# Storing two of 64 chunks in parts that run on different numbers of DMA engines

## The chip, the cores and the metric

The kernel runs on one core of one Trainium2 chip. The core has TensorE (PE, matmuls; its weight loads are listed as PEld), VectorE (DVE), ScalarE (ACT), GpSimd (POOL) and SyncE (SP), and 16 DMA engines that carry every transfer between HBM and the core's SBUF, whichever engine issued it. The metric is device time in microseconds (us), the median of three runs. One further execution was recorded by the hardware profiler; the durations in this document come from it.

## The reference

The input `x` is one image of 512 x 512 pixels with 192 channels in bf16, and the output has the same shape. The convolution has a 1 x 1 kernel, so each pixel is treated by itself: its 192 channels are four groups of 48, and each group is multiplied by its own 48 x 48 matrix.

```python
# k = 1, G = 4, Cg = 48, pad = 0
xg = x.reshape(B, H, W, G, Cg)
out = einsum('bhwgc,gcd->bhwgd', xg, w[0, 0])   # then back to (B, H, W, 192)
```

100.66 MB are read and as many written; the arithmetic beside them is small.

## The kernel before

**Chunks.** The 262,144 pixels are cut into 64 chunks of 4096 pixels. In a chunk each of the 128 SBUF partitions holds 32 neighbouring pixels, so one partition's row is 32 x 192 bf16 values, 12,288 bytes, contiguous in HBM. A chunk is 128 rows, 1.5 MB. Chunk n uses buffer n mod 5 of the five input buffers `x_sb` and of the five output buffers `o_sb`.

**Loads.** SP issues one load per chunk (L160), in order. From the sixth on, the load of chunk n first waits until PE has transposed all of chunk n-5, which was in the same buffer.

**Compute.** A chunk is worked in eight groups of four pixels per partition. PE transposes a group (six transposes, L192), DVE copies them from PSUM to SBUF (L242), PE multiplies by a block-diagonal weight (six matmuls, L214), and ACT writes the result to `o_sb` as bf16 (L285); in three groups of ten DVE and ACT do one half each (L249, L282). PE runs up to two groups of transposes ahead. The weights are built at the start from `w`.

**Stores.** ACT issues one store per chunk (L269), in `store(n)`, after the chunk's last group. ACT's program is in order and has this shape: at the first group of chunk n it waits until the store of chunk n-5 has landed on all its DMA engines (`st_sem`), and the store of chunk n-1 comes after that, two groups into chunk n. So the store of chunk n-1 is not issued before that of chunk n-5 has landed. DVE waits on the same semaphore before it first writes `o_sb` for a chunk.

**Queues.** Loads are on the queue called q1, stores on q10. A chunk's 128 rows are dealt out evenly, eight to each of the 16 DMA engines, and each engine counts the semaphore up by one when its rows are done; a whole transfer counts 16. `store_parts(n)` already allows a store to be made in several transfers; before the change it returns one part of 128 rows for every chunk.

Of the kernel before, what the change touches and what calls it, by code (L numbers as in the profile page):

```python
# [24 lines left out]
PPC = 32  # L25
NB = 5
TAIL = (32, 32, 32, 32)
RELIEF = ()
RELIEF_ROWS = ((0, 128),)
NXP = 4  # L30
NOB = 4
NXS = 4
# [21 lines left out]
def bass_standalone__grouped__vision_kernel(nc, x, w, out):  # L54
# [49 lines left out]
        return ap[pix0[n]:pix0[n] + 128 * s, :].rearrange("(p i) c -> p (i c)", p=128)  # L104

    def store_parts(n):
        return RELIEF_ROWS if n in RELIEF else ((0, 128),)

    st_total, acc = [], [0] * NB
    for n in range(n_chunks):  # L110
        acc[n % NB] += 16 * len(store_parts(n))
        st_total.append(acc[n % NB])
# [4 lines left out]
    with ExitStack() as es:  # L117
# [136 lines left out]
        def _(act):  # L254
# [4 lines left out]
            def store(n):  # L259
                b = n % NB  # L260
                g = g1[n] - 1
                if g < GT:
                    wq.wait(mm_done, g + 3)
                else:
                    wq.wait(actT_sem, actT_cnt(g))
                    wq.wait(ev2T_sem, dveT_cnt(g))
                dst = rows_view(of, n)
                for (r0, r1) in store_parts(n):
                    act.dma_start(dst[r0:r1, :], o_sb[b][r0:r1, 0:sizes[n] * C]).then_inc(st_sem[b], 16)  # L269
# [51 lines left out]
```

## Time and profile before

| | us |
|---|---|
| median of three runs | 494.51 (491.5, 494.51, 494.85) |
| the profiled execution's own time | 494.62 |
| its span, first to last instruction | 492.9 |
| PE / ACT / DVE busy | 415.4 / 349.0 / 348.0 |
| packets of q1 and q10, share of 16 engines' span | 48.3% and 48.2% |
| mean rate over the span | 409 GB/s |

The span is 1.7 us shorter than the execution's own time. A "packet" is what one DMA engine moves at a time: here one row of 12,288 bytes, or the 4-byte count of the semaphore.

The trace also records when each of the 16 engines counted its part of a transfer as done. These are some transfers, in us from the start of the span, with the engines sorted by the time at which they were done (the trace does not give the engines' numbers):

| transfer | issued | first engine | 9th | 15th | last engine |
|---|---|---|---|---|---|
| store of chunk 20 | 155.56 | 177.45 | 178.49 | 179.91 | 184.93 |
| store of chunk 42 | 322.55 | 338.38 | 339.42 | 341.64 | 353.13 |
| store of chunk 45 | 345.52 | 360.30 | 361.32 | 363.57 | 376.09 |
| load of chunk 51 | 348.96 | 363.99 | 364.62 | 367.25 | 379.92 |
| store of chunk 57 | 437.27 | 448.09 | 449.10 | 451.99 | 467.76 |
| load of chunk 63 | 440.53 | 451.31 | 452.40 | 455.68 | 471.52 |
| store of chunk 58 | 444.94 | 453.61 | 454.25 | 457.51 | 473.56 |
| store of chunk 62 | 474.35 | 479.24 | 479.35 | 479.86 | 488.68 |
| store of chunk 63 | 480.45 | 485.34 | 485.45 | 485.53 | 492.31 |

A column is read downwards: how fast that engine advances. A row is read across: how far the engines are apart.

### The profile page before, as it was taken

To read this page: it belongs to the slowest core of one execution; us is meant where nothing else is said; L and a number is where in the kernel's file an instruction comes from. 1 tells how busy PE (TensorE), PEld (TensorE's weight loads), DVE (VectorE), ACT (ScalarE), POOL (GpSimd) and SP (SyncE) were. 2 spreads that over 40 slices of the span, in tenths; PEclk is the share of its full clock that TensorE was granted. 3 is DMA by queue.
4 is the path that set the end of the run, shared out by engine and by line. 5 is a ranking of instruction groups with operands and counts; after the bars stand their busy time and mean duration, and the time that the engine had idled before them with its cause. 6 is when DMAs were issued, how large, how long until landed. Compare 5 with 4: busy or idle time off the path is not lost.

```text
span 492.9 us, 15013 instructions
## 1 busy us (share of the span) xinstructions
PE 415.4 (84%) x6154; PEld 390.5 (79%) x6154; DVE 348.0 (71%) x666; ACT 349.0 (71%) x513; POOL 1.3 (0%) x8
## 2 busy tenths in 40 slices
PE   4888999999999888888888888888888888888880
PEld 4788999999989887787777877878778787787770
DVE  2767888888888776776776767677667767777760
ACT  1757888888888767677677776766767667676680
POOL 1000000000000000000000000000000000000000
PEclk9989999999999999999999999999999999999995
DMA  8999999999999999999999999999999999999563
GB/s 342 398 428 426 427 429 427 428 428 428 429 428 429 430 429 430 429 430 428 427 430 430 429 429 429 430 428 427 429 428 430 428 427 430 430 430 430 213 266 144
DMA packets 18658, 201.56 MB, mean 409 GB/s; under 512 B 2256, under 2 KB 2256, under 8 KB 2256
## 3 DMA queue, kind: packets, MB, share of 16 engines
q1 hardware_dynamic: 9424, 100.69, 48.3%
q10 hardware_dynamic: 9216, 100.67, 48.2%
q8 instruction: 7, 0.11, 0.1%
q14 instruction: 11, 0.09, 0.0%
HBM read 100.68 MB, written 100.66 MB: 409 GB/s over the span
## 4 chain that ended last, share of the span: by engine, by line
DMA 67%; PE 2%; ACT 1%; ACTq 0%; issue 0%
DMA out_dram<-o_sb 67%; PE o_ps L214 1%; ACT o_sb L285 1%; PE xT_ps L192 1%; ACTq L269 0%; ACT o_sb L282 0%; ACTq L47 0%
## 5 line engine op out<-in xcount | busy, mean ns | idle before, releaser
L285 ACT CAST o_sb<-o_ps 128x768 bf16<-128x768 f32 x359 | 280.1, 799 | 99.9 <-PE o_ps L214 65.4
L242 DVE COPY xT_sb<-xT_ps 128x768 bf16<-128x768 bf16 x512 | 282.3, 554 | 89.4 <-PE xT_ps L192 84.3
L214 PE MATMUL o_ps<-wt,xT_sb 128*128 128x144 bf16 (+1 forms) x3072 | 297.5, 233 | 46.9 <-PEq L169 40.5
L192 PE MATMUL xT_ps<-ident,x_sb 128*128 128x128 bf16 x3072 | 256.7, 220 | 10.0 <-PEq L169 4.9
L214 PEld LDWEIGHTS o_ps<-wt,xT_sb 128*128 128x128 bf16 x3072 | 210.9, 98 | 64.4 <-issue 51.5
L192 PEld LDWEIGHTS xT_ps<-ident,x_sb 128*128 128x128 bf16 x3072 | 196.8, 98 | 17.2 <-issue 17.1
L249 DVE CAST o_sb<-o_ps 128x384 bf16<-128x384 f32 x153 | 84.6, 553 | 32.9 <-DMA out_dram<-o_sb 20.0
L282 ACT CAST o_sb<-o_ps 128x384 bf16<-128x384 f32 x153 | 73.4, 480 | 30.7 <-DMA out_dram<-o_sb 19.6
L178 PE MATMUL o_ps<-w_sb,esel 48*128 48x48 bf16 x10 | 0.6, 209 | 7.3 <-DMA w_sb<-in_w_dram 7.3
L236 DVE CAST wt<-o_ps 128x480 bf16<-128x480 f32 x1 | 0.7, 658 | 7.9 <-PE o_ps L178 7.9
L178 PEld LDWEIGHTS o_ps<-w_sb,esel 48*128 48x128 bf16 x10 | 0.5, 110 | 7.3 <-issue 7.3
L285 ACT ACT_TABLE_LOAD x1 | 1.3, 1283 | 0.9 <-PEq L306 0.9
L145 POOL TENSOR_SCALAR_AFFINE_SELECT esel<-esel 48x272 bf16<-48x272 bf16 x1 | 0.4, 406 | 0.0
L142 POOL MEMSET esel<- 48x272 bf16 x1 | 0.3, 318 | 0.3 <-POOLq L306 0.3
L149 POOL TENSOR_SCALAR_AFFINE_SELECT ident<-ident 128x128 bf16<-128x128 bf16 x1 | 0.3, 286 | 0.0
L143 POOL MEMSET ident<- 128x128 bf16 x1 | 0.2, 198 | 0.0
L306 POOL MEMSET const-bfloat16-1.0<- 128x1 bf16 x1 | 0.1, 102 | 0.0
L306 POOL MEMSET const-uint8-127<- 128x1 uint8 x1 | 0.1, 102 | 0.0
L306 POOL MEMSET const-float32-1.0<- 128x1 f32 x1 | 0.1, 99 | 0.0
L306 POOL MEMSET const-float32-0.0<- 128x1 f32 x1 | 0.1, 98 | 0.3 <-issue 0.3
## 6 DMA issues: line engine op xcount, KB each, us to landing
x_sb<-in_x_dram SPq DMA_DIRECT2D x64, 1536.0 KB, 30.9
out_dram<-o_sb ACTq DMA_DIRECT2D x64, 1536.0 KB, 30.5
w_sb<-in_w_dram SPq DMA_DIRECT2D x1, 18.0 KB, 5.9
```

Of the source, the lines that this page charges most:

```text
L142: gp.memset(esel[:], 1.0).then_inc(p0_sem, 1)
L145: gp.affine_select(out=esel[:], in_=esel[:], pattern=[[-1, ECOLS]], compare_op=AluOpType.is_equal, fill=0.0, base=ESHIFT, channel_multipli ...
L149: gp.affine_select(out=ident[:], in_=ident[:], pattern=[[-1, 128]], compare_op=AluOpType.is_equal, fill=0.0, base=0, channel_multiplier=1) ...
L178: last = pe.matmul(o_ps[:, NOB - 1, col:col + CG], lhsT=esel[:, s0:s0 + 128], rhs=w_sb[:, g, :], start=True, stop=True, skip_group_check=True)
L192: last = pe.transpose(xT_ps[:, g % NXP, j * 128:(j + 1) * 128], x_sb[b][:, col:col + 128], ident[:])
L214: last = pe.matmul(o_ps[:, v, c0:c1], lhsT=xs[:, j * 128:(j + 1) * 128], rhs=wt[:, WOFF[tc]:WOFF[tc] + (c1 - c0)], start=(tc == 0), stop=( ...
L236: dve.tensor_copy(wt[:], o_ps[:, NOB - 1, 0:WCOLS]).then_inc(wc_sem, 1)
L242: dve.tensor_copy(xT_sb[g % NXS][:], xT_ps[:, g % NXP, 0:2 * UC]).then_inc(ev1_sem, 1)
L249: dve.tensor_copy(o_sb[n % NB][:, u * UC:(u + 1) * UC], o_ps[:, (2 * g + 1) % NOB, 0:UC]).then_inc(ev2_sem if g < GT else ev2T_sem, 1)
L282: ins = act.copy(ob[:, u * UC:(u + 1) * UC], o_ps[:, v, 0:UC])
L285: ins = act.copy(dst, o_ps[:, v:v + 2, 0:UC])
L306: nc = _bacc.Bacc("TRN2", target_bir_lowering=False, num_devices=1)
```

## The change

The stores of chunks 20 and 42 are made in parts; all others stay one transfer of 128 rows. The rows of a part are neighbouring partitions, and every part is its own DMA on ACT's queue that counts 16 on the same semaphore; the waits (`st_total`, L109 on) count the parts.

- Chunk 20: parts of 48, 76 and 4 rows. The 48 go to all 16 engines (three each), the 76 and the 4 to the first four engines (19 and one each).
- Chunk 42: parts of 48, 68, 5, 6 and 1 rows. The 48 go to all 16 engines, the 68 to the first four (17 each), and the last twelve rows to the first five, the first six and the first one, one row each.

Six more DMAs are issued in all. The bytes, the loads, the compute and the order of everything else are unchanged.

```diff
-RELIEF = ()
-RELIEF_ROWS = ((0, 128),)
+RELIEF = {20: (48, 76, 4), 42: (48, 68, 5, 6, 1)}
...
     def store_parts(n):
-        return RELIEF_ROWS if n in RELIEF else ((0, 128),)
+        parts, r = [], 0
+        for rows in RELIEF.get(n, (128,)):
+            parts.append((r, r + rows))
+            r += rows
+        assert r == 128
+        return parts
```

## The prediction

> **What bounds the kernel now.** I read the page's slices and queues first, then the chain that ended last, the waits, and stretches of the tail.
>
> The slices and queues of the page:
>
> ```profile
> DMA  8999999999999999999999999999999999999563
> ...
> q1 hardware_dynamic: 9424, 100.69, 48.3%
> q10 hardware_dynamic: 9216, 100.67, 48.2%
> ```
>
> The 16 DMA engines are full in all but the last three slices. PE, the busiest compute engine, has 84%. The queues are equally large: 9216 packets are 64 stores of 128 rows and 16 counts.
>
> The chain that ended last (start us, duration us, what):
>
> ```profile
> 345.52 30.57 DMA out_dram<-o_sb
> 376.12 30.56 DMA out_dram<-o_sb
> 406.71 30.53 DMA out_dram<-o_sb
> 437.27 30.49 DMA out_dram<-o_sb
> ```
>
> The chain is stores, each issued as the one four chunks earlier lands. Four chunks take 30.6 us, so one takes 7.64.
>
> Stretches of the tail (window; length; busy us and count of PE, PEld, DVE, ACT, POOL; clock; DMA share; GB/s):
>
> ```profile
> 452.00:456.00 4.00, 2.98 (x49) 2.81 (x47) 2.69 (x6) 3.14 (x5) 0.00 (x0) 1.00 1.01 427
> 464.00:468.00 4.00, 3.71 (x58) 3.42 (x55) 3.52 (x8) 2.10 (x4) 0.00 (x0) 1.00 0.19 77
> 485.50:487.00 1.50, 0.00 (x0) 0.00 (x0) 0.00 (x0) 0.00 (x0) 0.00 (x0) 0.50 0.06 25
> 489.00:490.00 1.00, 0.00 (x0) 0.00 (x0) 0.00 (x0) 0.00 (x0) 0.00 (x0) 0.50 0.06 25
> ```
>
> This carries the reading. From 485.5 us nothing computes and the DMA share is 0.06, one sixteenth: **one engine works and fifteen have finished.** The table of completions says why. From the store of chunk 20 to that of chunk 57 the first engine advances from 177.45 to 448.09, 270.64 us for 37 chunks, or 0.457 us a row (a chunk is eight rows loaded and eight stored); the last one from 184.93 to 467.76, 282.83 us, or 0.478 us a row. This slow engine loses 0.33 us each chunk and is 15.8 us behind the 15th at chunk 57. It never runs dry, so the end is the sum of its own rows.
>
> The waits (us in total, times, longest):
>
> ```profile
> ACT o_sb L285 <- DMA out_dram<-o_sb: 30.9, 25, 1.9
> DVE o_sb L249 <- DMA out_dram<-o_sb: 20.0, 24, 1.2
> ```
>
> ACT and DVE wait for landed stores in every chunk of the second half: these are waits for the slow engine.
>
> **The change, part by part.**
>
> *Rows taken away.* In chunk 20 an engine outside the first six stores 3 rows instead of 8, in chunk 42 the same. That is 10 rows x 0.478 = **4.78 us** off the slow engine if it is one of these. In the tail, where the others have stopped, it does a row in 0.457 (488.68 to 492.31 for eight); at that price it would be 4.6. I take 4.78, because both chunks lie where all engines are busy.
>
> *Rows added.* Engine 0 stores 3+19+1 = 23 rows in chunk 20 and 3+17+1+1+1 = 23 in chunk 42: 30 more than before. Engines 1 to 3 get 29 more. At 0.457 that is 13.7 and 13.3 us. The cover: when the 9th engine has landed store 58 (454.25) its loads are over and five stores of eight rows remain, 40 x 0.457 = 18.3 us; fed without a gap it would be done at 472.5, the 15th at 457.51 + 18.3 = 475.8. Adding 13.7 gives **486.2 and 489.5**. The slow engine lands at 492.31 - 4.78 = **487.5**. So the four stay just beneath the new end, unless they include the one or two that are furthest behind (then up to 2 us later).
>
> *Price of a row on the four.* No transfer of the trace uses only some engines. Nearest rows: 0.457 and 0.478 in the steady part; at the other end, the first packets of the first load took 0.69 to 1.14 us each. With 30 rows on 472.5 the four reach 487.5 at 0.50 us a row and the old end, 492.31, at 0.66. I take 0.457, the row of thousands of packets, and keep both ends for the range.
>
> *Six more issues on ACT.* One takes 0.34 us (L269, ACT's queue), so 0.7 us at chunk 20 and 1.4 at chunk 42. Behind them in ACT's order stand the evictions of the next chunk, for which PE waits. ACT waits about 1.2 us per eviction after a landed store (30.9 / 25), and the store issues at the period of the DMA anyway, so I cost it at nothing; uncovered it is 2.0 us at most.
>
> *The new wait.* The extra rows go behind others in the four engines' store queue, and while loads are queued too the queues take turns (0.914 us per stored row). Store 20 lands on the four 15 x 0.914 = 13.7 us later than 177.45, at about 191.2 instead of 184.93. The store of chunk 24 is issued 6.3 us late, and chunk 25's evictions, the matmuls behind them and load 30 are late with it. Until chunk 42 the four set the pace, at 7.31 us a chunk rather than 7.64, which returns 0.33 us x 18 = 6 us of it. Chunk 42 then adds 15 rows to a queue that is already 15 rows late: it lands on the four at about 338.4 + 13.7 + 13.7 = 365.8 instead of 353.13, 12.7 us late. Store 46 and, some 3.5 us after, load 52 are late by the same.
>
> Does the slow engine run dry in this pause? Its stores up to 45 are landed at 376.09 - 9.6 = 366.5, its load 51 would land at 379.9, as before. At 365.8 it has about 14 us of loads left when taking turns, 7 us alone, and store 46 comes now. It stays busy, with **some 7 us to spare**. The ordinary engines do run dry for some 4 us, which they can afford (they are some 15 us ahead). After the pause compute is free to run at its own pace: store 8 to store 18 were issued 6.53 us apart (76.85 and 142.19), with PE busy 97% of the time between 50 and 150 us, so store 63 could be issued at 365.8 + 17 x 6.55 = 477, no later than now (480.45); the slow engine needs it by 482.6 (487.1 - 3.65 - 0.8). So the pause costs nothing, with 2 to 5 us in hand there.
>
> *Sum.* 494.62 - 4.78 = **489.8 us**, 0.97% less. Profiled time and median (494.51) differ by 0.1, so the same figure stands for the median.
>
> [...]
>
> **Rivals.**
>
> 1. *The four finish last.* If a row costs them 0.50 to 0.66 us, or the ones furthest behind are among them, the end is between 487.5 and 492.3, the time 490 to 494.6. Against it: steady packets hardly vary. For it: they have only 1 us to spare. I price it at 491.5.
> 2. *The slow engine is one of the first four* (slower than before). It then gains 29 or 30 rows, 29 x 0.478 = 13.9 us, and the time is 508.5. It decides as soon as its number is 0 to 3. By count alone that is 4 in 16. What speaks against it: in the last store fifteen idle engines begin 0.84 to 0.99 us after the issue, mostly 2 to 23 ns apart, with one gap of 29 ns between the 6th and the 7th; if they are served in order of number, the slow one, busy at that time, belongs there. That is an inference.
> 3. *The four cost more still, or the pause outlasts the slow engine's backlog.* Each us beyond the 7 is a us at the end; at twice the price of a row (0.91) the four end at 472.5 + 27.4 = 499.9, the time is 502.
> 4. *The parts use all engines after all.* Nothing moves: 494.6.
>
> **How the numbers follow.** The forecast has 0.60, its own range 488 to 491. Rival 1 has 0.24, rival 2 0.06, rival 3 0.06, rival 4 0.04. The runs of the kernel before lie 3.4 us apart (0.7%), so about 1% is what a measurement can tell from no change; 1% is 489.56 here, just beside the forecast. Of the forecast's 0.60 I put 0.36 beyond it and 0.24 within; with rivals 1 and 4 within 1% has 0.52, and rivals 2 and 3 make 0.12 slower. The range runs from 487.4 (a slow engine that is itself a little faster, as the run of 491.5 suggests, with the four as the next bound: 486.2 + 0.6 + 1.7 = 488.5, less a little) to 495, the end of rivals 1 and 4; some 0.15 is left out, nearly all of it above.
>
> **What would show it.** In the profile after: the last stretch at a share of 0.06 short or gone, the share at or above 0.25 until the end; the landing of store 20 near 191 and of store 42 near 366; a dip of the DMA share near 362 to 370; the last landing near 487.5; waits of ACT and DVE for stores longer at chunks 25 and 47 and gone afterwards. It is wrong if the share is 0.06 for longer than before (rival 2), 0.25 for the last 5 us or more (rivals 1 and 3), or if the slow engine shows a gap near 370 to 375.

## The result: slower, and the profile after

The change makes the kernel slower: 498.91 us median of six runs (498.67 to 500.66) against 493.34 (491.50 to 494.85, six runs, with the three shown earlier among them), ratio 1.0131 with a 95% interval of 1.0105 to 1.0156. The prediction was 489.8, reckoned from the profiled execution of the kernel before, 494.62. Medians in this document are over all runs of a kernel, while ratios leave out runs more than 1.5% above its fastest, so where a kernel's times scatter the two differ. The profiled execution took 499.01 us, its span is 497.2; the last store lands at 496.63 on the profile's clock, 4.3 us later than before instead of 4.8 earlier.

The page's slices and the store queue after:

```profile
DMA  8999999999999999999999999999938999999985
GB/s 341 396 425 429 428 428 428 426 428 432 429 429 426 426 423 416 425 427 427 431 428 428 428 430 429 422 414 405 402 146 330 376 428 430 427 427 429 428 368 219
...
q10 hardware_dynamic: 9240, 100.67, 48.0%
```

A slice is 12.4 us. Where before every slice from the third up to 450 us had about 428 GB/s, there is now a slow decline from 310 us on (422, 414, 405, 402), a hole of 146 GB/s near 365 us, and two slices of recovery. The queue has 24 packets more than the 9216 of before. That is what the counts should add if the parts run on 16, 4, 5, 6 and 1 engines: 16 + 4 + 4 for chunk 20 and 16 + 4 + 5 + 6 + 1 for chunk 42, less 2 x 16; the semaphores show 24 counts for the first of these stores and 32 for the second. The trace does not number the engines.

Stretches of the profile after (window; length; busy us and count of PE, PEld, DVE, ACT, POOL; clock; DMA share; GB/s):

```profile
310.00:355.00 45.00, 40.69 (x615) 38.98 (x613) 34.56 (x67) 34.39 (x51) 0.00 (x0) 0.99 1.01 414
355.00:373.00 18.00, 1.88 (x30) 1.67 (x27) 1.41 (x3) 0.80 (x1) 0.00 (x0) 0.70 0.54 220
373.00:390.00 17.00, 15.74 (x204) 15.19 (x204) 11.78 (x23) 12.32 (x18) 0.00 (x0) 0.82 0.88 348
390.00:440.00 50.00, 48.49 (x734) 46.37 (x735) 41.39 (x80) 41.52 (x63) 0.00 (x0) 1.00 1.01 419
493.00:494.00 1.00, 0.00 (x0) 0.00 (x0) 0.00 (x0) 0.00 (x0) 0.00 (x0) 0.50 0.14 61
494.00:496.00 2.00, 0.00 (x0) 0.00 (x0) 0.00 (x0) 0.00 (x0) 0.00 (x0) 0.50 0.07 31
```

For 18 us PE does 1.88 us of work. Afterwards PE is busy 97% of the time: the DMA is no longer what it waits for, its own pace is. At the end two engines (0.14) and then one (0.07) work alone, but now for some 3 us and not 6. In the first row the share is 1.01 as before while the rate is 414 and not 429: the engines are as busy and move less. That row matters below.

ACT's part of the hole, from the timeline (start us, us, instruction, idle before it and what ended that), and the wait in the table of waits:

```profile
355.03 0.80 ACT L289 CAST o_sb<-o_ps 128x768 bf16<-128x768 f32 x1 [0.33 <-PE o_ps L218]
373.03 0.80 ACT L289 CAST o_sb<-o_ps 128x768 bf16<-128x768 f32 x1 [17.20 <-DMA out_dram<-o_sb]
373.04 0.34 ACTq L273 DMA_DIRECT2D out_dram<-o_sb  x1
```

```profile
ACT o_sb L289 <- DMA out_dram<-o_sb: 41.8, 15, 17.2
DVE o_sb L253 <- DMA out_dram<-o_sb: 26.0, 11, 16.4
```

ACT waits 17.2 us for the store of chunk 42 before it may write chunk 47. The completions in the trace say which engines it waits for. Eleven of the others have done their three rows of that store by 335.2. Of the four that the part of 68 rows runs on two are done by 365.7 and **two only at 372.7 and 373.0**. Chunk 43's store tells the same pairs: 369.2 and 369.7, 376.4 and 377.2. Stores 47 to 57 are then issued from 382.39 to 447.81, 6.54 us apart, which is PE's pace, and the last store is issued at 488.23 instead of 480.45. Even the first engine lands that at 493.12, 4.89 us after the issue, past the old end of 492.31; the two late ones land it at 495.13 and 496.63. That these are the later pair of the four is read from the order in which stores land, since the trace gives no engine's number.

### The profile page after: what moved, and what is told of

Its sections match the earlier page's. It is cut to its first block, busy times and chain, and to the rows that moved or that the text cites. A ratio compares the mean times of both kernels' runs of the same rounds, so it can differ in the third digit from the quotient of the medians.

```text
span 497.2 us, 15019 instructions
## 1 busy us (share of the span) xinstructions
PE 413.4 (83%) x6154; PEld 394.3 (79%) x6154; DVE 347.9 (70%) x666; ACT 349.3 (70%) x513; POOL 1.3 (0%) x8
## 5 line engine op out<-in xcount | busy, mean ns | idle before, releaser
L196 PEld LDWEIGHTS xT_ps<-ident,x_sb 128*128 128x128 bf16 x3072 | 199.2, 99 | 8.4 <-issue 8.2
```

What stands on the lines that cost most here:

```text
L196: last = pe.transpose(xT_ps[:, g % NXP, j * 128:(j + 1) * 128], x_sb[b][:, col:col + 128], ident[:])
```

## The experiments

All are compared with the kernel before, run on the same chip beside them. A "dose" is one store made in parts. "Long rows" are the packets of whole rows on the store queue that took over 0.6 us, and their sum is what they took beyond 0.46 us each; the kernel before has 3.5 us of them in the whole run and 1.4 us from 60 us on. The changed kernel has 8.5 us of them between the first issue and the landing of store 20 and 8.8 us in the same stretch of store 42.

**One dose at a time.** First theory (A): the wait of 17.2 us is what costs. Its rival (B): the rows on the four engines cost too much.

```diff
-RELIEF = {20: (48, 76, 4), 42: (48, 68, 5, 6, 1)}
+RELIEF = {20: (48, 76, 4)}
```

> Only chunk 20 is stored in parts (48, 76, 4); chunk 42 is stored whole. Theory A (the wait of 17.2 us for the store of chunk 42 is what costs: it empties the queues, after it the compute's own pace of 6.55 us a chunk sets the end): with one dose the wait at chunk 25 is about 9 us, as in the changed kernel, and the queues are long enough to bridge it. The slow engine is then relieved of 5 rows and nothing else changes: 2.4 us less than the kernel before, ratio 0.995. Theory B (rows on the first four engines cost more than 0.457 us and these engines set the end by their sum): half of what the change lost, about 2.8 us more than before, ratio 1.006.

Measured: 491.59 us, ratio 0.9984 (0.9966 to 1.0003). ACT's longest wait is 9.6 us, long rows 6.2 us at this dose. One engine alone works at the end, as before (a share of 0.06 from 485.6 us on). Neither 0.995 nor 1.006: the pause was bridged, and little was gained.

```diff
-RELIEF = {20: (48, 76, 4), 42: (48, 68, 5, 6, 1)}
+RELIEF = {42: (48, 68, 5, 6, 1)}
```

> Only chunk 42 is stored in parts (48, 68, 5, 6, 1); chunk 20 is stored whole. Theory A: without the first dose the four engines come to chunk 42 with 15 rows less in their queues, so its store lands near 352 to 356 us and ACT's longest wait is 1 to 4 us instead of 17.2; time 2.4 us less than before, ratio 0.995. Theory B: about 2.8 us more than before, ratio 1.006. If instead the whole loss comes again with this dose alone (ratio 1.011), the place of the dose, not the sum of both, is to blame.

Measured: 493.87 us, ratio 1.0036 (1.0010 to 1.0061), near B's figure. ACT's waits for stores in this run:

```profile
ACT o_sb L289 <- DMA out_dram<-o_sb: 21.8, 8, 12.9
```

One dose, on queues that were not late, still makes a wait of 12.9 us where A had 1 to 4. The trace shows what is added there: 22.3 us of long rows between 330 and 360 us. One of the four engines takes 1.68, 1.89, 1.07, 1.93 and 2.48 us for some of its rows, while the loads between them take 0.46. At store 41 all engines but the slow one are within 4.5 us of each other (330.2 to 334.7); the four land store 43 at 359.8, 360.6, 366.6 and 371.9.

**The same rows in small doses.**

```diff
-RELIEF = {20: (48, 76, 4), 42: (48, 68, 5, 6, 1)}
+RELIEF = {n: (112, 4, 4, 4, 4) for n in range(12, 52, 4)}
```

> The same rows are moved between the same engines, but in ten small doses: the stores of chunks 12, 16, ... 48 are made of parts of 112 rows (seven per engine) and four times 4 rows (one each on the first four). Every engine from the fifth on stores 10 rows less in all, the first four 30 more, nearly as in the change, with 3 rows at a time instead of 15. Theory A: no wait over about 4 us, and the time that the prediction gave, some 4 us less than before: 489 to 490, ratio 0.991. Theory B: the sums per engine are the same, so the time is that of the changed kernel, 499, ratio 1.011. 40 more issues on ACT of 0.34 us each are expected to hide in ACT's waits in both.

Measured: 514.29 us, ratio 1.0342 (1.0278 to 1.0406), worse than either theory. There are 119 us of long store rows. And a cost that both took for nothing appears, ACT held up in issuing DMAs (the waits; "issue" is time in which an engine waits for nothing that the profile shows):

```profile
ACT o_sb L289 <- issue: 23.4, 23, 8.2
```

This line is 2.6 us in all and 0.4 at most in the kernel before. The last store is issued only at 508.0 us and lands on the first engine at 512.9, on the last at 515.1, so the run does not separate A from B.

**Which engine is slow.**

```diff
-RELIEF = {20: (48, 76, 4), 42: (48, 68, 5, 6, 1)}
+RELIEF = {20: (120, 8), 30: (120, 8), 40: (120, 8), 50: (112, 7, 8, 1)}
```

> Which engine is the slow one? The stores of chunks 20, 30 and 40 are made of 120 rows (eight each on the first fifteen engines) and 8 rows (one each on the first eight); engine 15 stores nothing of them. Chunk 50 is stored as 112 rows on all, then 7, 8 and 1 rows on the first seven, eight and one engines. If the slow engine is number 15, it is relieved of 25 rows, 25 x 0.478 = 12 us, while eight engines gain 4 rows (2 us): the time falls to about 482, ratio 0.976. If it is one of 8 to 14 the time stays (1.000), if it is one of 0 to 7 it grows by about 2 us (1.004). In the latter two cases the parts of 7 and 8 rows of chunk 50 tell: the one that holds the slow engine has one completion some 10 us behind the others.

Measured: 501.21 us, ratio 1.0202 (1.0144 to 1.0261): none of the three. But the completions answer the question. Of chunk 50's store the last three come at 419.8, 420.7 and 422.1, the one before them at 406.6: the engine that is late holds a row of the parts of 112, 7 and 8, and not of the part of 1, so its number is 1 to 6 if parts run on the engines from 0 upward. In the changed kernel the slow engine counts the store of chunk 42 at 342.5, 343.4 and 344.9, three parts: 48, and those of 5 and 6 rows, but not the 68. On that condition, which the counts fit and no run shows, it is **engine 4**, and the change gave it two rows back: 8 are taken off it and not 10. There are 33 us of long rows in this run, so splitting goes with long rows here too, where no engine stores more than two rows beyond its eight in a store.

**Doses behind which nobody waits.**

```diff
-RELIEF = {20: (48, 76, 4), 42: (48, 68, 5, 6, 1)}
+RELIEF = {59: (48, 76, 4), 61: (48, 76, 4)}
```

> Two doses of 48, 76 and 4 rows, but in the stores of chunks 59 and 61, whose buffers nobody waits for any more, instead of chunks 20 and 42. Theory A (the wait behind the parts costs, the moved rows gain): without any wait the slow engine's end comes 10 rows x 0.457 = 4.6 us earlier, and the first four, idle between stores by then, end at about 486.4 on the clock of the profile before, plus what their rows take over 0.457 us (two of them up to 6 us more, by the rows of 0.8 to 2.6 us seen in the runs before this one): 488 to 492 in all, ratio 0.990 to 0.998. Theory B (the four engines' rows in parts of k = 4 cost so much that they are last anyway): 493 or more, ratio over 1.000.

Measured: 499.63 us, ratio 1.0139 (1.0099 to 1.0178), with 61 us of long rows between 450 and 490. Nobody waits for a buffer here and the loss is as large as that of the change, so the wait of theory A is not needed for it. But the run does not decide for B either, because a third cost stands in it, ACT held in issuing the parts (a line of the waits and one of ACT's timeline):

```profile
ACT o_sb L289 <- issue: 16.3, 26, 6.4
468.12 6.23 ACTq L273 DMA_DIRECT2D out_dram<-o_sb  x3
```

The three issues of chunk 61's store take 6.23 us. The last store is issued at 488.77 us instead of 480.45; the first engine lands it at 493.7, the last at 497.15. What held ACT is open.

**Eight output buffers.** The wait is taken away by giving `o_sb` and `st_sem` eight buffers; the first run is the base without parts.

```diff
+NSB = 8
-        o_sb = [... for i in range(NB)]
+        o_sb = [... for i in range(NSB)]
 # and n % NSB for o_sb, st_sem, acc and st_before throughout
-RELIEF = {20: (48, 76, 4), 42: (48, 68, 5, 6, 1)}
+RELIEF = {}          # first run; the second keeps the change's parts
```

> The kernel before with eight output buffers instead of five (no store in parts): chunk n waits for the store of chunk n-8. The slow engine works without a break in both, so the time should stay: ratio 1.000, at most 0.5% either way. It is the base for the next run.

> The changed kernel (chunks 20 and 42 in parts) with eight output buffers instead of five: the same parts, but chunk 50 and not chunk 47 waits for the store of chunk 42, some 22 us later. Theory A: ACT's longest wait for a store falls from 17.2 us to under 3 us, the DMA engines do not run empty, and the slow engine, relieved of 8 rows, sets the end: 490 to 492, ratio to the kernel before 0.993 to 0.998. Theory B: with the wait gone the four engines' extra rows still make them last, about 499, ratio 1.010.

Measured: the base 492.33 us, ratio 0.9998 (0.9979 to 1.0016), as expected. With the parts 500.57 us, ratio 1.0104 (1.0061 to 1.0148), in ten runs from 494.7 to 507.8. Stretches and waits of the run with parts:

```profile
345.00:380.00 35.00, 27.30 (x393) 25.77 (x394) 22.55 (x43) 22.24 (x33) 0.00 (x0) 0.94 1.01 415
488.00:492.00 4.00, 0.00 (x0) 0.00 (x0) 0.00 (x0) 0.00 (x0) 0.00 (x0) 0.50 0.13 55
492.00:495.00 3.00, 0.00 (x0) 0.00 (x0) 0.00 (x0) 0.00 (x0) 0.00 (x0) 0.50 0.12 53
```

```profile
ACT o_sb L290 <- DMA out_dram<-o_sb: 12.1, 7, 4.5
```

The long wait is gone (4.5 us at most), there is no hole in the DMA (1.01), and the time is no better. From 488 us on two engines of 16 work alone, a share of 0.13. The last store's completions tell which, by the order in which the engines follow one another from store to store: five engines end after the rest, at 485.48, 486.01 and 487.19 (the slow one and two of the four), and at **496.72 and 497.02**. These two were some 10 us behind the other two of the four from the parts of chunk 42 on (they land store 43 at 383.9 and 384.1, the others at 372.6 and 374.1), and while those parts were stored the trace has 15.6 us of long rows. The last store is issued at 477.32, so nothing held the end up but these two. The part of 68 rows of chunk 42, 17 rows to an engine, took two of the four engines some 15 us, as 17 x 0.914 = 15.5 has it, and these two 21 to 24 us. So the chain of theory A is not what decides. The rows of the part on four engines are, and they do not cost the same on all four.

**What makes rows long.** Four runs move no row from one engine to another in number.

```diff
-RELIEF = {20: (48, 76, 4), 42: (48, 68, 5, 6, 1)}
+RELIEF = {20: (64, 64), 42: (64, 64)}
```

> The stores of chunks 20 and 42 are made of two parts of 64 rows, so that every engine still stores eight rows but four and four of other partitions than before, and no engine gets more than another. If the long store rows (0.6 to 2.6 us instead of 0.46) come from splitting a store or from an engine reading other partitions than in a whole store, they appear here too, some 5 to 20 us of them in all; if they need parts that run on few engines, this looks like the kernel before: under 2 us of them, and the time of the kernel before within 1%.

Measured in one run: 495.46 us, 11.3 us of long rows in the two stores (7.7 and 3.6). So a part need not run on few engines to have them.

```diff
 def store_parts(n):      # (rows of the output, partitions of o_sb)
+    if n in (20, 26, 32, 38, 44, 50):
+        near = [slice(16 * r, 16 * r + 16) for r in range(8)]
+        wide = [slice(r, 128, 8) for r in range(8)]
+        return zip(near, near)   # near;  zip(wide, wide): every eighth row;  zip(near, wide): mixed
```

> Where do long store rows come from? Six stores (chunks 20, 26, 32, 38, 44, 50) are made of eight parts of 16 neighbouring rows. Every engine still stores eight rows of each, one of each part, so no engine is relieved; but if a whole store gives engine i the rows 8i to 8i+7, as the two parts of 64 rows suggest, each engine now reads partitions, and writes places in HBM, that other engines use at the same time. Theory C (long rows come from an engine storing rows that another engine's loads and stores work on): long rows of 0.6 us and more in each of the six stores, 5 to 20 us of them for each, some 30 to 120 in all, and the time 1 to 3% above the kernel before. Theory D (they come from splitting as such, from more DMAs and counts): the same as in the next run.

> The same six stores in eight parts of 16 rows, but each part takes every eighth row (r, r+8, ... r+120), so that engine i again stores just the rows 8i to 8i+7. Theory C: no long rows (under 3 us in all, as in the kernel before), the time of the kernel before, ratio 1.000, up to 1.004 for 42 more issues on ACT. Theory D: as many long rows as with parts of neighbouring rows.

> As the run before, each engine reads its own eight partitions, but the rows are written to 16 neighbouring places in HBM, so that only the place written is another engine's (the output has the rows of these six chunks in another order). If the place read in SBUF is what makes rows long, there are none here, as with every eighth row; if the place written in HBM does, there are as many as with neighbouring rows.

| | long store rows from 60 us on | ACT held in issuing: in all, longest | ratio |
|---|---|---|---|
| parts of neighbouring rows | 98.5 us | 37.5, 12.6 | 1.0108 (1.0068 to 1.0148) |
| every eighth row | 25.1 us | 34.4, 9.1 | 1.0125 (1.0081 to 1.0168) |
| every eighth partition to neighbouring places in HBM | 29.8 us | 43.3, 11.0 | 1.0149 (1.0107 to 1.0192) |

The long rows behave as theory C has it, though not down to nothing: which partitions a part is made of changes them more than three-fold (98.5 us to 25.1 and 29.8), which places in HBM it writes hardly at all (25.1 to 29.8). Each sum is from one traced execution, and single stores have from 5 to 35 us with neighbouring rows and 0.7 to 11.4 in the other two. That a whole store gives engine i the rows 8i to 8i+7 is assumed in these runs; no trace shows it. The times do not follow. The last store is issued at 491.6, 489.1 and 494.6 us (480.45 before), in the order of what ACT loses in issuing 48 small DMAs, so that rather than the long rows seems to set them:

```profile
154.19 5.05 ACTq L270 DMA_DIRECT2D out_dram<-o_sb  x8
159.28 1.50 ACT L286 CAST o_sb<-o_ps 128x768 bf16<-128x768 f32 x2 [4.94 <-issue]
```

Eight issues take 5.05 us instead of 8 x 0.34 (this is the run with every eighth row). The eviction behind them waits 4.94 us, and PE behind that (its longest wait before the matmuls of L215 is 8.9 us in this run, 1.1 in the kernel before). What in the choice of partitions lies behind the three sums above, no run here shows.

**Place or form of the dose.** Both with eight output buffers.

```diff
-RELIEF = {20: (48, 76, 4), 42: (48, 68, 5, 6, 1)}
+RELIEF = {14: (48, 76, 4), 24: (48, 76, 4)}              # first run
+RELIEF = {20: (48, 68, 5, 6, 1), 42: (48, 76, 4)}        # second run
```

> Eight output buffers, and the two doses of 48, 76 and 4 rows at chunks 14 and 24 instead of 20 and 42. The slow engine stores 10 rows less, 4.8 us; the first four 30 more. If the long rows belong to a late dose or to the form of the second one (48, 68, 5, 6, 1), there are under 15 us of them here in both doses together, the four engines end near 487 to 489 and the time is 490 to 491.5, ratio 0.995 to 0.998: faster than both kernels. If every dose on four engines makes two of them lose some 8 to 10 us whatever its place and form, the time is again 498 to 502, ratio 1.012.

> As the changed kernel with eight output buffers, but the forms change places: chunk 20 is stored as 48, 68, 5, 6, 1 and chunk 42 as 48, 76, 4. If the place makes the long rows, those at chunk 42 stay (10 us and more) and the time stays near 500, ratio 1.010; if the form does, they move to chunk 20 and chunk 42 has under 8 us of them, with about the same time.

Measured: 501.84 us, ratio 1.0133 (1.0066 to 1.0201), and 503.88 us, from 496.2 to 507.4. Long rows by dose: 5.6 us at chunk 14 and 31 at chunk 24, both of the first form; 23.7 us at chunk 20 in the second form and 6.8 at chunk 42 in the first. Neither place nor form orders these sums. In both runs, as with eight buffers above, two engines end long after the rest, at 497.4 and 501.0 and at 496.6 and 499.2, while the last store was issued at 481.3 and 479.2. What decides how much a dose loses is left open; none of the versions with parts beats the kernel before clear of noise.

## Why the prediction was wrong

- **The failing step: "Price of a row on the four."** I took 0.457 us, "the row of thousands of packets", for a form that the trace did not contain, and named 0.69 to 1.14 as the other end. The price differs between the four. In the part of 68 rows two of them took 21 to 24 us with eight buffers, where 15.5 was to be expected, so, with a load row of 0.457 after each, 0.8 to 1.0 us a row instead of 0.457; in the change itself they took 17.6 and 19.4, and the other two about 15 in both. In the run with only chunk 42 in parts the 22.3 us of long rows are, spread over the 68 rows, up to 0.33 us each, so up to 0.79 us a row on the mean of the four; in the change itself the means are below 0.6 and it is the uneven share that counts. With eight buffers two of the four ended at 496.7 and 497.0, past the old end of 492.3. Rival 1 reached that end at 0.66 us a row; two of the four past it are rival 3, the four costing more still, to which I gave 0.06 (0.30 with rival 1). The arithmetic around the price holds: by 0.457 us a row the four were to end at 486.2 to 489.5, and the two without many long rows ended between 485.5 and 487.2.
- **"So the pause costs nothing" failed as well.** The store of chunk 42 landed at 373.0 and not 365.8, 19.9 us later than before instead of 12.7, and ACT waited 17.2 us for it. I started from the first engine's landing, but ACT waits for the last of the four (landed at 373.01, ACT went on at 373.03). At store 41 the prediction's way gives 331.03 + 13.7 = 344.7 (331.03 is the first engine in the trace before); measured are 343.6 to 349.6. The other 2.3 us came in the second dose itself. The 2 to 5 us that I had in hand for compute were thereby gone: store 63 was issued at 488.23, past the 482.6 that I had named as the limit. Compute's pace of 6.54 us was right. By this alone the end would be at 493.1, 0.8 us later than before. But the run with eight buffers shows that without this pause the time is no better, so it is a second loss beside the first; how the loss of the change divides between the two is not shown.
- **"10 rows" are 8.** I excluded the first six engines by an inference from a gap of 29 ns in the start times; the slow one is engine 4, if parts run on the engines from 0 upward, and the parts of 5 and 6 rows each gave it a row. The gain to be had was 3.8 us. Rival 2, the slow engine among the first four, did not come true, by one number; that was luck, as the inference had put it behind the sixth.
- **Right:** the reading that one engine sets the end of the kernel before, and that parts run on 16, 4, 5, 6 and 1 engines (no transfer in the trace before runs on fewer than 16, so how many rows each engine gains or loses was an assumption; the 24 counts more bear out how many engines a part runs on, and no run shows that these are the first ones); the first dose, which landed at 194.1 for 191.2 and was bridged (ratio 0.998 alone); the six issues, whose cost did hide in the change (0.4 us at most in ACT's order), though two stores of three parts at chunks 59 and 61 held ACT for up to 6.4 us.
- Beyond the six issues the prediction gave splitting itself no cost. Two halves of 64 rows, which make 16 counts each, have 11.3 us of long rows, and 64 whole stores have 3.5.

## What to carry to other kernels

An imbalance between DMA engines can be seen (a share of 0.06, one sixteenth, at the end), but rows that are moved by splitting a transfer can cost more: here single rows of the parts took up to 2.6 us instead of 0.46 (only chunk 42 in parts). Measure the price of such a row in one small run before summing with it. Here the release by a semaphore came with the last engine (373.01, and ACT went on at 373.03): a forecast for a group of engines starts from the slowest of the group.

## What the runs showed of the hardware that I had not expected

- A row of 12,288 bytes on the store queue, 0.46 us in a whole store, took up to 2.6 us in a part of a store, while load rows on the same engine in between stayed at 0.46 us (only chunk 42 in parts).
- The sum of such rows changes from dose to dose without visible order, from none (chunk 20 with eight buffers, where the same parts had 8.5 us with five) to 31 us. The time of one and the same kernel goes from 494.7 to 507.8 us with eight buffers; that the long rows make this scatter is likely and not shown, as one execution of it was traced.
- One of 16 engines, number 4 if the parts run on the engines from 0 upward, takes 0.478 us a row where the others take 0.457, as long as the others are busy; in the tail, alone, it took 0.454 (488.68 to 492.31 for eight, kernel before).
- ACT, which issues a store in 0.34 us, is held up to 12.6 us in issuing when a store is made of eight DMAs, and up to 6.4 us with three.
